# K and V in whole-group transfers, the first x tiles transposed on TensorE, and loads moved at a block change

## The chip, the core and the metric

The kernel runs on one core of one Trainium2 chip. The metric is the device time of one execution in microseconds (us). Engines are named as the profile names them: PE is TensorE (PEld its weight loads), DVE is VectorE, ACT is ScalarE, POOL is GpSimd, SP is SyncE. SP issues every DMA of this kernel from one queue (q1 on the page of the kernel before, 161.12 of the 162.59 MB moved; the rest is instructions), in program order; "SPq" is that queue.

## The reference

Two independent attention blocks, A and B, of the same shape. Each projects x to queries, attends to a cached K and V, and projects back; the two results stand side by side in the output.

```python
# for each of the two blocks; all inputs bf16
B, Sq, D = 8, 144, 640          # batches, queries per batch, model width
H, Sk, Dh = 32, 512, 128        # heads, cached keys, head width
q = (x @ wq).reshape(B, Sq, H, Dh).transpose(0, 2, 1, 3)
scores = einsum("bhqd,bhkd->bhqk", q, k_cache) * Dh ** -0.5
p = softmax(scores)
o = einsum("bhqk,bhkd->bhqd", p, v_cache)
out = o.transpose(0, 2, 1, 3).reshape(B, Sq, H * Dh) @ wo
# result: concatenate([out_A, out_B], axis=-1)
```

K and V are the bulk of the data: 8 x 32 x 512 x 128 bf16 elements, 33.5 MB each for each block.

## The kernel before

The work is cut into 64 **groups**, numbered 0 to 63: one batch, eight heads. Groups 0 to 31 are block A, 32 to 63 block B. For a group, PE projects x to queries, computes the scores (144 queries are 128 "main" and 16 "remainder"; the remainders of all eight heads share one tile), DVE and ACT do the softmax, PE transposes the probabilities, multiplies with V, and later multiplies with wo. Projections by wo ("out-projection") serve as filler between the steps of later groups.

The program declares each operation with what it reads and writes. A static scheduler in the same file then orders every engine's instructions before the program is built. So an edit to the loads can also move instructions on the compute engines.

Every load goes to SP. x is needed transposed, and the DMA transposes it; so is K. K and V come four heads at a time:

```python
NK = 4      # K buffers of 4 heads each
NV = 6      # V buffers of 4 heads each

def load_xT(blk, half):             # half of the 1152 tokens: 576
    ...
    for c in range(NCH):            # NCH = 5 slices of 128 of D = 640
        def f(e, c=c):
            return e.dma_start_transpose(xT_sb[:, c, t0:t1], xf[t0:t1, c * 128:(c + 1) * 128])
        S.add("sp", f, writes=[("xT", half, c)], ...)

def load_kv(blk, b, g):
    for s2 in range(2):             # two 512 KB chunks for K, two for V
        h0 = 8 * g + 4 * s2
        kslot = kv_ctr[0] % NK
        vslot = kv_ctr[0] % NV
        ...
        ksrc = kc[b, h0:h0 + 4].rearrange("h k d -> (h k) d")
        vsrc = vc[b, h0:h0 + 4].rearrange("h (p c) d -> p h (c d)", p=128)
        # K: dma_start_transpose(kt_sb[:, kslot, :], ksrc); V: dma_start(v_sb[:, vslot], vsrc)
```

This is when the other loads are issued (`before(g, f)` puts load f ahead of group g):

```python
before(0, lambda: load_xT(0, 0))                  # A's first x half, first of all
before(0, lambda: load_wq(0, 0))                  # then a quarter of A's wq
for g in range(1, NG):
    before(g, lambda g=g: load_wq(0, g))
...
for blk in range(2):
    for b in range(NB):
        ...
        for g in range(NG):
            attention_group(blk, b, g, gi, fill, heads_done)
            gi += 1
            if blk == 0 and b == NB - 1:
                load_wq(1, g)                     # B's wq, a quarter after each of A's last groups
        if blk == 0 and XH == 2 and b == BPH - 1:
            load_xT(1, 0)
        if blk == 0 and b == NB - 1:
            load_xT(1, XH - 1)                    # B's second x half, exactly at the block change
            queues[0].extend(outproj_ops(blk, NB))
            for hg in range(NHG):                 # B's four wo quarters, all after A's last out-projection
                queues[0].append((1, -1, 0, None, lambda hg=hg: do_load_wo(1, hg), NB - 1))
```

## Time and profile before

| what | value | where it is read |
|---|---|---|
| time, median of the 4 runs known then | 789.9 us (786.13 to 790.65) | the runs |
| PE busy | 747.3 us of a span of 787.2 us | the page, part 1 |
| PE busy, 25 to 100 us | 65.46 of 75 us, DMA at 264 GB/s | busy time by windows |
| PE busy, 375 to 400 us (block change) | 20.69 of 25 us | busy time by windows |
| PE busy, 450 to 475 us (B's wo) | 23.04 of 25 us | busy time by windows |
| first projection matmul | 13.67 us | timeline of PE |

The page of the kernel before, its span, its first part (busy time of each engine, share of the span, instructions) and its fourth (shares of the chain of waits that ended last):

```profile
span 787.2 us, 23122 instructions
PE 747.3 (95%) x9088; PEld 565.6 (72%) x9088; DVE 719.9 (91%) x1858; ACT 613.1 (78%) x1957; POOL 0.7 (0%) x6
PE 84%; DMA 9%; DVE 4%; SPq 1%; ACT 1%; issue 0%; ACTq 0%
```

PE bounds the kernel as a whole. Only about 40 us of the span are idle on PE, and they lie in a few places. The windows view of the kernel before shows those places. Its columns are the stretch in us and its length, then the busy time and instruction count of PE, PEld, DVE, ACT and POOL, then the granted clock of PE as a share of full speed, the DMA share, and the GB/s moved:

```profile
25.00:100.00 75.00, 65.46 (x782) 48.54 (x783) 66.14 (x170) 56.12 (x179) 0.00 (x0) 0.98 1.11 264
375.00:400.00 25.00, 20.69 (x236) 14.81 (x235) 20.44 (x55) 17.32 (x55) 0.00 (x0) 0.97 1.09 235
450.00:475.00 25.00, 23.04 (x249) 15.99 (x247) 19.89 (x51) 17.27 (x57) 0.00 (x0) 1.00 1.07 273
```

The longest waits of PE, from the waits view of the kernel before (who waited for what: us in total, times, longest):

```profile
PE ps_q L396 <- DMA wq_sb<-in_A_wq_dram: 13.7, 1, 13.7
PE ps_s L425 <- DMA kt_sb<-in_B_k_cache_dram: 5.4, 2, 4.3
```

Why these two are long is in the timeline of the SP queue (start, how long the issue held the queue, operation, what it moves, how many). At the start five transposes of x hold the queue before wq gets its turn; at the block change five more hold it for 10.24 us before B's first K:

```profile
0.80 6.46 SPq L315 DMA_TRANSPOSE xT_sb<-in_A_x_dram  x5
7.31 0.58 SPq L294 DMA_DIRECT2D wq_sb<-in_A_wq_dram  x1
7.94 5.48 SPq L335 DMA_TRANSPOSE kt_sb<-in_A_k_cache_dram  x1
...
380.39 10.24 SPq L315 DMA_TRANSPOSE xT_sb<-in_B_x_dram  x5
390.73 5.51 SPq L335 DMA_TRANSPOSE kt_sb<-in_B_k_cache_dram  x2
```

A good clock for progress is the burst of eight small "remainder" score matmuls, one burst per group.

Groups 40 to 60 took 11.3 us each. In groups 0 to 8, K landed only 0.0 to 2.5 us before the scores that read it; later about 6.5 us before. So the first 120 us run at the pace of the DMA, and the rest does not.

### The profile page before, as it was taken

The page shows a single profiled execution, that of the slowest core. Times are in us where ns is not written, and L with a number is a line of the kernel's source. Part 1 is how long each engine was busy: PE and PEld are TensorE (multiplying, and loading weights), DVE is VectorE, ACT ScalarE, POOL GpSimd, SP SyncE. Part 2 cuts the span into 40 slices and gives each one's busy share as a digit, 9 for nine tenths or more (in the row PEclk, how much of TensorE's full clock was granted, in tenths as well). Part 3 has the DMA queues.
Part 4 walks back from the last instruction along what each step waited for, and adds up shares of the span by engine and source line. Part 5 has one row for each costly group of instructions (what it writes and reads, how often), then busy time and mean ns, then how long its engine had stood idle before and what let it go on. Part 6 is the DMA issues. An engine that isn't in the chain of part 4 may idle for free.

```text
span 787.2 us, 23122 instructions
## 1 busy us (share of the span) xinstructions
PE 747.3 (95%) x9088; PEld 565.6 (72%) x9088; DVE 719.9 (91%) x1858; ACT 613.1 (78%) x1957; POOL 0.7 (0%) x6
## 2 busy tenths in 40 slices
PE   2789899999999999999979999999999999999997
PEld 1567667778777777778757767777777778787864
DVE  2799899989999999999969879999999999999992
ACT  1678678778888888888868768888888888888873
POOL 0000000000000000000000000000000000000000
PEclk9999999999999999999999999999999999999999
DMA  7999999998999888899999899988989787889820
GB/s 185 285 236 292 253 253 231 215 230 192 200 221 194 192 196 190 188 229 272 235 227 230 234 267 244 217 186 196 192 190 192 196 185 199 189 194 194 188 34 18
DMA packets 362476, 162.59 MB, mean 207 GB/s; under 512 B 281216, under 2 KB 357248, under 8 KB 362368
## 3 DMA queue, kind: packets, MB, share of 16 engines
q1 hardware_dynamic: 362368, 161.12, 91.2%
q8 instruction: 72, 1.18, 0.7%
q14 instruction: 36, 0.29, 0.1%
HBM read 88.08 MB, written 2.95 MB: 116 GB/s over the span
## 4 chain that ended last, share of the span: by engine, by line
PE 84%; DMA 9%; DVE 4%; SPq 1%; ACT 1%; issue 0%; ACTq 0%
PE ps_q L396 19%; PE ps_o L531 15%; PE ps_out L578 14%; PE ps_pt L504 13%; PE ps_s L483 13%; DMA kt_sb<-in_A_k_cache_dram 5%; PE ps_s L425 4%; PE ps_out L593 4%; DMA kt_sb<-in_B_k_cache_dram 2%; DVE nm_sb L355 2%; PE ps_pt L450 2%; PE ps_q L578 1%; DMA wo_sb<-in_B_wo_dram 1%; DMA wq_sb<-in_A_wq_dram 1%; SPq L315 1%; DVE p_sb L376 1%
## 5 line engine op out<-in xcount | busy, mean ns | idle before, releaser
L359 ACT ACTIVATE p_sb<-ps_s,nm_sb 128x512 bf16<-128x512 f32 x576 | 397.2, 696 | 59.5 <-DVE nm_sb L355 44.2
L355 DVE TENSOR_REDUCE nm_sb<-ps_s 128x1 f32<-128x512 f32 x576 | 383.7, 678 | 26.2 <-PE ps_s L483 17.2
L396 PE MATMUL ps_q<-xT_sb,wq_sb 128*128 128x144 bf16 x2560 | 205.2, 228 | 15.4 <-DMA wq_sb<-in_A_wq_dram 13.7
L396 PEld LDWEIGHTS ps_q<-xT_sb,wq_sb 128*128 128x128 bf16 x2560 | 173.2, 99 | 50.3 <-DMA wq_sb<-in_A_wq_dram 13.7
L520 DVE COPY ptg_sb<-ps_pt 128x1024 bf16<-128x1024 bf16 x256 | 174.7, 685 | 21.6 <-PE ps_pt L504 19.2
L483 PE MATMUL ps_s<-kt_sb,qt_sb 128*128 128x512 bf16 x512 | 184.6, 382 | 7.6 <-ACT p_sb L359 4.3
L376 DVE TENSOR_SCALAR p_sb<-p_sb,rr_sb 128x512 bf16<-128x512 bf16 x576 | 180.2, 345 | 1.4
L531 PE MATMUL ps_o<-ptg_sb,v_sb 128*128 128x144 bf16 x2048 | 171.3, 227 | 0.7 <-DVE ptg_sb L465 0.4
L531 PEld LDWEIGHTS ps_o<-ptg_sb,v_sb 128*128 128x128 bf16 x2048 | 138.8, 98 | 35.8 <-DVE ptg_sb L520 10.8
L504 PE MATMUL ps_pt<-id_sb,p_sb 128*128 128x128 bf16 x2048 | 156.0, 220 | 2.9 <-DVE p_sb L376 2.8
L504 PEld LDWEIGHTS ps_pt<-id_sb,p_sb 128*128 128x128 bf16 x2048 | 132.0, 114 | 24.0 <-DVE p_sb L376 10.7
L407 ACT ACTIVATE qt_sb<-ps_q 128x288 bf16<-128x288 f32 x256 | 106.7, 417 | 53.3 <-PE ps_q L396 50.3
L578 PE MATMUL ps_out<-wo_sb,otm_sb 128*128 128x512 bf16 x512 | 131.4, 379 | 0.9 <-DMA wo_sb<-in_B_wo_dram 0.9
L544 ACT CAST otm_sb<-ps_o 128x256 bf16<-128x256 f32 x256 | 94.9, 371 | 45.9 <-PE ps_o L531 42.1
L359 ACT ACTIVATION_READ_ACCUMULATOR p_sb<-ps_s,nm_sb 128x1 f32 x576 | 120.3, 209 | 0.0
L578 PEld LDWEIGHTS ps_out<-wo_sb,otm_sb 128*128 128x128 bf16 x512 | 48.5, 98 | 44.9 <-issue 1.3
L483 PEld LDWEIGHTS ps_s<-kt_sb,qt_sb 128*128 128x128 bf16 x512 | 47.6, 98 | 24.5 <-ACT p_sb L359 10.4
L371 DVE RECIPROCAL rr_sb<-rs_sb 128x2 f32<-128x2 f32 (+1 forms) x320 | 49.9, 156 | 3.3 <-ACT p_sb L359 2.5
L545 ACT CAST otr_sb<-ps_o 128x32 bf16<-128x32 f32 x256 | 50.4, 197 | 0.0
L425 PE MATMUL ps_s<-kt_sb,qt_sb 128*32 128x512 bf16 x512 | 39.8, 388 | 5.9 <-DMA kt_sb<-in_B_k_cache_dram 5.4
L593 PE MATMUL ps_out<-wo_sb,otm_sb 128*128 128x128 bf16 x512 | 38.8, 219 | 0.0
L593 PEld LDWEIGHTS ps_out<-wo_sb,otm_sb 128*128 128x128 bf16 x512 | 32.3, 98 | 7.4 <-issue 2.5
(25 smaller groups left out, 135.9 us busy)
## 6 DMA issues: line engine op xcount, KB each, us to landing
v_sb<-in_A_v_cache_dram SPq DMA_DIRECT2D x64, 512.0 KB, 4.4
v_sb<-in_B_v_cache_dram SPq DMA_DIRECT2D x64, 512.0 KB, 4.4
wq_sb<-in_A_wq_dram SPq DMA_DIRECT2D x4, 1280.0 KB, 7.5
wo_sb<-in_A_wo_dram SPq DMA_DIRECT2D x4, 1280.0 KB, 8.2
wq_sb<-in_B_wq_dram SPq DMA_DIRECT2D x4, 1280.0 KB, 7.5
wo_sb<-in_B_wo_dram SPq DMA_DIRECT2D x4, 1280.0 KB, 8.2
out_dram<-ost_sb SPq DMA_DIRECT2D x16, 160.0 KB, 3.6
kt_sb<-in_A_k_cache_dram SPq DMA_TRANSPOSE x64, 5.9
```

Of the source, the lines that this page charges most:

```text
L355: return v.tensor_reduce(nm_sb[:, ts:ts + 1], ps_s[:, sbank, :], AXL.X, ALU.max, negate=True)
L359: return a.activation(p_sb[:, pslot, :], ps_s[:, sbank, :], ACTF.Exp, bias=nm_sb[:, ts:ts + 1], scale=1.0, accum_out=rs_sb[:, ts:ts + 1])
L376: return v.tensor_scalar(p_sb[:, pslot, :], p_sb[:, pslot, :], rr_sb[:, ts:ts + 1], None, ALU.mult)
L396: ins = t.matmul(ps_q[:, uu * SQ:(uu + 1) * SQ], wq_sb[:, c, h * 128:(h + 1) * 128], xT_sb[:, c, b * SQ:(b + 1) * SQ], start=(c == 0), sto ...
L407: return a.mul(qt_sb[:, gs, 2 * pi:2 * pi + 2, off:off + SQ], ps_q[:, 0:2 * SQ].rearrange("p (u q) -> p u q", u=2), SCALE,)
L483: return t.matmul(ps_s[:, sbank, :], qt_sb[:, gs, u, qoff:qoff + 128], kt_sb[:, slot, (u % 4) * SK:(u % 4 + 1) * SK], start=True, stop=True,)
L504: ins = t.transpose(ps_pt[:, kpt, (uu * 4 + c) * 128:(uu * 4 + c + 1) * 128], pv[:, c, :], id_sb[:],)
L520: return v.tensor_copy(dst, src)
L531: ins = t.matmul(ps_o[:, uu * SQ:(uu + 1) * SQ], v_sb[:, slot, u % 4, c * 128:(c + 1) * 128], ptg_sb[:, gs, u, c, :], start=(c == 0), stop ...
L544: a.copy(otm_sb[:, bs, h0:h0 + 2, :], src[:, :, 0:128])
L578: ins = t.matmul(acc[:, 0:512], lhs(h), wo_sb[:, h, 0:512], start=(h == 0), stop=(h == H - 1))
L593: ins = t.matmul(acc[:, 0:D2], lhs(h), wo_sb[:, h, 512:D], start=(h == 0), stop=(h == H - 1))
```

## The change

It has three parts that can be switched separately, and I use letters for them:

- **X**: the first 256 tokens of A's x come by one plain DMA (320 KB) and are transposed on PE, so that wq need not wait behind five DMA transposes. The other 320 tokens of the half still come by five DMA transposes, but after the first K and V.
- **K**: K and V come eight heads (1 MB) at a time, in two K and three V buffers of twice the size. The total buffer size stays.
- **R**: loads of B are retimed. B's second x half moves 12 groups later in the program (from the block change to group 44), B's wq quarters one group later, and each wo quarter of B is issued right after A's last reader of the old one rather than all four at the end. The scheduler then places them: in the SP queue of the changed kernel the x half stands before and after K of group 40, and of the wq quarters only the last has changed its place, to behind K of group 32.

A third output staging buffer, checks at build time that a buffer holds what is expected, and a new semaphore numbering of the DMAs come with it. The cut diff:

```diff
+KV_HEADS = 8
+NK, NV = 2, 3
+NOS = 3
+WQB_LEAD = 2
+XT_PE_TILES = 2
 ...
-    NK = 4
-    NV = 6
-    NOS = 2
 ...
+        def load_x_pe():
+            # one plain DMA of 256 tokens into the output staging buffer, then
+            # ten PE transposes by the identity and two evictions by DVE
+            ...
+                        ins = t_.transpose(ps_pt[:, kpt, j * 128:(j + 1) * 128],
+                                           stage[:, t, c * 128:(c + 1) * 128], id_sb[:])
 ...
-            for s2 in range(2):
-                h0 = 8 * g + 4 * s2
+            for s2 in range(8 // KV_HEADS):
+                h0 = 8 * g + KV_HEADS * s2
 ...
-        before(0, lambda: load_xT(0, 0))
-        before(0, lambda: load_wq(0, 0))
+        if NXA:
+            before(0, load_x_pe)
+            before(0, lambda: load_wq(0, 0))
+            if BPH * SQ > NXA:
+                before(1, lambda: load_xT(0, 0, skip=NXA))
 ...
+        for g in range(NG):
+            before(max(last_g[(0, g)] + 1, first_g[(1, g)] - WQB_LEAD), lambda g=g: load_wq(1, g))
+        if XH == 2:
+            before(max(last_half[(0, 1)] + 1, first_half[(1, 1)] - NG), lambda: load_xT(1, 1))
 ...
-                    if blk == 0 and b == NB - 1:
-                        load_wq(1, g)
-                if blk == 0 and b == NB - 1:
-                    load_xT(1, XH - 1)
 ...
+                for k, it in enumerate(passb):
+                    queues[0].append(it)
+                    for hg in range(NHG):
+                        if ((hg + 1) * 8 - 1) // OPB_HEADS == k:
+                            queues[0].append((1, -1, 0, None, lambda hg=hg: do_load_wo(1, hg), NB - 1))
```

With every switch of the changed kernel set back, the program that it builds has the same instructions and waits, in the same order on every engine, as the kernel before. So X, K and R are the whole of the change.

## The prediction

> **What bounds the kernel now.** TensorE: the page gives PE 95% busy, and the chain of waits is 84% PE. The windows table shows three regimes.
> - To 125 us: DMA bound. The first matmul starts at 13.67 us, after a 13.7 us wait on A's wq. From 25 to 125 us the DMA share is 1.10 to 1.16 at 244 to 276 GB/s, PE is busy 21.0 to 23.9 of 25 us, and groups of 8 heads (timeline, one remainder-score burst each) are mostly 11.9 to 13.6 us apart.
> - 125 to 750 us: PE bound, 25.0 of 25 us; late groups are 11.3 us apart; DMA 180 to 210 GB/s.
> - Two dents: 375 to 400 us (PE 20.7 of 25, a 4.3 us wait on K), where transposes of B's second x half stand before K in the queue (380 to 390 us), and 450 to 475 us (PE 23.0), where B's four wo loads do.
>
> Counting matmul starts later than their line's median, the excess over steady state is about 38 us up to 125 us, 5 us at the block change, 2 us at wo.
>
> **What the change does.**
> 1. First x: five 576-token DMA transposes (issued 0.8 to 7.3 us) become one plain 320 KB load, ten PE transposes (about 56 ns each) and evictions (about 0.7 us each, DVE idle). wq goes second instead of sixth and should land near 8 us, not 13.6. The other 320 tokens still go through the transposing DMA, behind K and V. Estimate: 4 to 5 us gained; the DMA-bound stage ends that much earlier, and this reaches the kernel's end.
> 2. K and V in 1 MB transfers. [...] Here the 512 KB transfers already stand back to back on saturated engines: I expect 0 to 3 us. The price: K of group i+2 starts only when all scores of group i are done. Now K's second half lands about 6.5 us before its scores in steady state; a 1 MB K takes about 2.5 us longer, so slack falls to 2 to 5 us: free in steady state, thin where weights load.
> 3. B's second x half moves 12 groups later, B's wq one or two groups, each B wo follows its last reader. The block-change stall nearly goes, but wq adds about 4 us of DMA to each of four groups with thin K slack: net 2 to 4 us. The four wo still stand before one, now whole, K: 0, give or take 2.
> 4. A third output buffer and the buffer assertions: nothing.
>
> PE work[...] is unchanged; the gain is removed idle time: 4.5 + 1 + 3 = about 8 us.
>
> **Predicted:** 782 us, 774 to 788 eight times in ten. Faster by over 2%: 0.16; within 2%: 0.81; slower by over 2%: 0.03.
>
> **What would show it.** Step 1: first projection matmul near 8 to 9 us, first scores near 14 instead of 16.7; A's wo loads end 3 to 6 us before the 104.3 of now. Step 2: unchanged 250 to 275 GB/s from 25 to 100 us; PE still 25.0 of 25 in steady state. Step 3: no x transposes near 385 us; the wait on B's K under 2 us; PE over 23 of 25 us in 375 to 400.
>
> **What would make it wrong.** If 1 MB transfers raise the saturated DMA rate, groups 0 to 8 shorten by about 1 us each and the gain passes 15 us. If the two whole-group K slots arrive late (waits on K every group), or an in-order V or wo issue blocks K, it is slower. If the rebuilt static order is worse on PE, 0.1 us per group is 6 us.

4.5 + 1 + 3 comes to 8.5, called about 8 us, and leads from 789.9 to 782 us. The 1 of step 2 was a guess within its 0 to 3 us.

Where the other figures stand in the kernel before: its 128x128 PE transposes begin 56 ns apart (a burst of eight at 600.03 us, the next matmul at 600.48), and a DVE copy of 128x1024 takes 685 ns. The 2.5 us are an estimate, from the 2.6 us (median) for which a 512 KB transpose of B's K holds the queue. The 4 us are one too: 1280 KB of wq at the 338 GB/s moved from 450 to 462 us, where wo quarters of the same size load, would take 3.9 us.

## More of the kernel before

In the timeline of PE of the kernel before, the first line is the first projection; the others are the bursts of groups 4, 8, 28 and 40:

```profile
13.67 1.38 PE L396 MATMUL ps_q<-xT_sb,wq_sb 128*128 128x144 bf16 x10 [13.67 <-DMA wq_sb<-in_A_wq_dram]
...
72.19 0.62 PE L425 MATMUL ps_s<-kt_sb,qt_sb 128*32 128x512 bf16 x8
...
120.86 0.61 PE L425 MATMUL ps_s<-kt_sb,qt_sb 128*32 128x512 bf16 x8
...
348.63 0.61 PE L425 MATMUL ps_s<-kt_sb,qt_sb 128*32 128x512 bf16 x8
...
498.65 0.61 PE L425 MATMUL ps_s<-kt_sb,qt_sb 128*32 128x512 bf16 x8
```

Groups 4 to 8 took 12.2 us each ((120.86 - 72.19) / 4).

## The result, and the profile after

The changed kernel took 781.73 us (median of 11 runs, 779.37 to 782.44), against 788.88 us for the kernel before (15 runs, 785.85 to 791.7). The ratio is 0.9903, with a 95% interval of 0.9888 to 0.9918. Here and below, a ratio is the mean time of one kernel's fast runs over the mean of the other's in the same rounds, so it is not quite the ratio of the medians that are quoted. When the same file was run again it took 779.34 us (4 runs) against 788.14 us, ratio 0.9891 [0.9867, 0.9915].

The page of the changed kernel, the same three lines:

```profile
span 779.8 us, 22892 instructions
PE 752.0 (96%) x9098; PEld 568.8 (73%) x9098; DVE 719.1 (92%) x1860; ACT 614.8 (79%) x1957; POOL 0.7 (0%) x6
PE 86%; DVE 7%; ACT 2%; DMA 2%; SPq 1%; issue 0%; ACTq 0%
```

PE has ten matmuls more (the x transposes) and is 7.4 us shorter in span. DMA fell from 9% of the last chain to 2%. The windows view of the changed kernel, the same stretches:

```profile
25.00:100.00 75.00, 67.14 (x806) 51.12 (x807) 66.67 (x172) 56.60 (x181) 0.00 (x0) 1.00 1.14 286
375.00:400.00 25.00, 25.00 (x299) 18.72 (x297) 24.22 (x67) 20.21 (x67) 0.00 (x0) 1.00 1.09 270
450.00:475.00 25.00, 24.24 (x277) 17.13 (x276) 16.96 (x47) 15.51 (x48) 0.00 (x0) 1.00 1.12 265
```

Two things stand out. The rate in the first window rose from 264 to 286 GB/s, which I had predicted not to happen. And the dent at the block change is gone: 25.00 of 25 us. The waits view of the changed kernel has for the same causes:

```profile
PE ps_q L465 <- DMA wq_sb<-in_A_wq_dram: 4.3, 1, 4.3
PE ps_pt L366 <- DMA ost_sb<-in_A_x_dram: 3.8, 1, 3.8
...
PE ps_s L498 <- DMA kt_sb<-in_B_k_cache_dram: 0.4, 1, 0.4
```

The timeline of the SP queue of the changed kernel, at the start and at the block change:

```profile
0.81 0.46 SPq L353 DMA_DIRECT2D ost_sb<-in_A_x_dram  x1
1.33 0.45 SPq L310 DMA_DIRECT2D wq_sb<-in_A_wq_dram  x1
1.83 9.06 SPq L396 DMA_TRANSPOSE kt_sb<-in_A_k_cache_dram  x1
...
11.56 6.41 SPq L341 DMA_TRANSPOSE xT_sb<-in_A_x_dram  x5
18.02 0.58 SPq L310 DMA_DIRECT2D wq_sb<-in_A_wq_dram  x1
...
378.99 5.30 SPq L396 DMA_TRANSPOSE kt_sb<-in_B_k_cache_dram  x1
384.34 0.57 SPq L310 DMA_DIRECT2D wq_sb<-in_B_wq_dram  x1
```

wq is issued at 1.33 instead of 7.31 us. But look at the x transposes: the five of 320 tokens hold the queue for 6.41 us, no less than the five of 576 tokens did before (6.46 us). X moved this time to a later place; it did not save it. (The five of 82 KB each stand behind a K and a V, the five of 147 KB stood on an empty queue. Whether the time is a cost per transfer or a queue that was full is open.)

The timeline of PE of the changed kernel, the first projection and the bursts of groups 4, 8, 28 and 40:

```profile
9.34 1.38 PE L465 MATMUL ps_q<-xT_sb,wq_sb 128*128 128x144 bf16 x10 [4.31 <-DMA wq_sb<-in_A_wq_dram]
...
69.61 0.61 PE L498 MATMUL ps_s<-kt_sb,qt_sb 128*32 128x512 bf16 x8
...
114.61 0.62 PE L498 MATMUL ps_s<-kt_sb,qt_sb 128*32 128x512 bf16 x8
...
345.85 0.61 PE L498 MATMUL ps_s<-kt_sb,qt_sb 128*32 128x512 bf16 x8
...
491.35 0.61 PE L498 MATMUL ps_s<-kt_sb,qt_sb 128*32 128x512 bf16 x8
```

The gain can be followed along the groups:

| burst of group | before | changed | earlier by | changed, run again | earlier by |
|---|---|---|---|---|---|
| 0 | 22.5 | 16.9 | 5.6 | 15.8 | 6.7 |
| 4 | 72.2 | 69.6 | 2.6 | 65.6 | 6.6 |
| 8 | 120.9 | 114.6 | 6.3 | 110.6 | 10.3 |
| 28 | 348.6 | 345.9 | 2.7 | 341.3 | 7.3 |
| 40 | 498.7 | 491.3 | 7.4 | 486.7 | 12.0 |
| end of span | 787.2 | 779.8 | 7.4 | 775.1 | 12.1 |

From group 4 to 8 the changed kernel takes 11.25 us a group, already its steady pace (groups 40 to 60: 11.3 us). Some 3 to 4 us of the lead at group 8 are gone at group 28. In the static order of the eight-head kernels about 2 us of work stands behind that mark instead of ahead of it (worked out from the durations of the instructions on both sides of the burst), so at least half of this is no loss. The same holds at groups 0 and 4, so the lead over the kernel before is smaller there than the table says. (Kernels with the same chunk size have the mark at the same place and can be compared directly.) After group 28 the block change and the wo loads bring another 4.7 us. Nothing is gained or lost after group 40.

The two traces of the same program differ by 4.7 us at the end, 4.0 us of it already at group 4. The section on the clock below comes back to that.

### The profile page after: what moved, and what is told of

It reads as the page before. It is cut to its first block, busy times and chain, and to the rows that moved or that the text cites. A ratio compares the mean times of both kernels' runs of the same rounds, so it can differ in the third digit from the quotient of the medians.

```text
span 779.8 us, 22892 instructions
## 1 busy us (share of the span) xinstructions
PE 752.0 (96%) x9098; PEld 568.8 (73%) x9098; DVE 719.1 (92%) x1860; ACT 614.8 (79%) x1957; POOL 0.7 (0%) x6
## 4 chain that ended last, share of the span: by engine, by line
PE 86%; DVE 7%; ACT 2%; DMA 2%; SPq 1%; issue 0%; ACTq 0%
PE ps_q L465 19%; PE ps_out L667 17%; PE ps_o L613 16%; PE ps_pt L582 14%; PE ps_s L559 13%; PE ps_s L498 5%; DVE nm_sb L415 4%; PE ps_pt L525 2%; ACT p_sb L420 2%; DVE p_sb L441 2%; DVE ptg_sb L594 1%; DMA kt_sb<-in_B_k_cache_dram 1%; PE ps_q L667 1%; DMA wq_sb<-in_A_wq_dram 1%; SPq L696 1%; DVE ptg_sb L536 0%
## 5 line engine op out<-in xcount | busy, mean ns | idle before, releaser
L667 PE MATMUL ps_out<-wo_sb,otm_sb 128*128 128x128 bf16 (+1 forms) x1024 | 170.1, 299 | 0.0
L582 PE MATMUL ps_pt<-id_sb,p_sb 128*128 128x128 bf16 x2048 | 157.8, 220 | 0.7 <-DVE p_sb L441 0.6
L536 DVE COPY ptg_sb<-ps_pt 128x256 bf16<-128x256 bf16 x128 | 30.8, 282 | 2.8 <-PE ps_pt L525 2.4
L525 PE MATMUL ps_pt<-id_sb,p_sb 128*128 128x128 bf16 x256 | 25.2, 221 | 1.0 <-DVE p_sb L441 1.0
```

The lines of the kernel that those rows point to most:

```text
L582: ins = t.transpose(ps_pt[:, kpt, (uu * 4 + c) * 128:(uu * 4 + c + 1) * 128], pv[:, c, :], id_sb[:],)
L667: ins = t.matmul(acc[:, 0:c1 - c0], lhs(h), wo_sb[:, h, c0:c1], start=(h == 0), stop=(h == H - 1))
```

## The experiments

Each experiment is an edit of the changed kernel unless said otherwise. The letters in the table say which parts are in. Kernels of one call share the runs of the kernel before, whose medians were 789.07, 790.71 and 788.14 us in calls 1, 2 and 3. The three calls ran on three different chips, so between calls only the ratios are compared. All were correct.

| kernel | parts in | call | median us | ratio to before [95%] |
|---|---|---|---|---|
| changed | X K R | first | 781.73 | 0.9903 [0.9888, 0.9918] |
| u_kv4 | X R | 1 | 784.43 | 0.9949 [0.9918, 0.9981] |
| u_xdma | K R | 1 | 786.21 | 0.9962 [0.9936, 0.9988] |
| u_noretime | X K | 1 | 784.86 | 0.9945 [0.992, 0.997] |
| u_xb | X K, R but for one load | 1 | 782.4 | 0.9909 [0.9883, 0.9935] |
| w_warm | X K R + warm-up | 2 | 784.91 | 0.9928 [0.9903, 0.9954] |
| w_late3 | X K R, rest of x later | 2 | 784.31 | 0.9925 [0.99, 0.995] |
| w_late3_warm | both | 2 | 784.77 | 0.9931 [0.991, 0.9953] |
| o_kv8 | K | 2 | 788.4 | 0.9974 [0.9951, 0.9997] |
| c_after | X K R (same file again) | 3 | 779.34 | 0.9891 [0.9867, 0.9915] |
| c_keep | X K R + filler matmuls | 3 | 780.27 | 0.9896 [0.9876, 0.9916] |
| c_late3_keep | rest of x later + filler matmuls | 3 | 782.0 | 0.9925 [0.9903, 0.9946] |
| o_x | X | 3 | 791.11 | 1.0039 [1.0015, 1.0063] |

My theory after the first look: X gives about what the trace shows at group 0; K gives something too, because the DMA rate rose; R removes the block-change stall. The rival to the first two: the start is bound by DMA anyway, so a lead from X is given back, and only the faster transfers of K count.

### u_kv4: the chunk size put back

```diff
-KV_HEADS = 8
-NK, NV = 2, 3
+KV_HEADS = 4
+NK, NV = 4, 6
```

> The changed kernel with K and V back in 4-head chunks (4 K slots, 6 V slots), all else as changed. Changed kernel: ratio 0.990 to before (781.7 us). Theory A (the gain is idle time taken out at the start by the PE-transposed x and at the block change by the later x half; the larger chunk adds little and costs K slack): 779 to 783 us, ratio 0.986 to 0.991; K lands again in halves, the last about 6.5 us before its remainder scores in steady state. Rival B (the 1 MB chunk is what pays: DMA moved 280 to 291 GB/s from 25 to 100 us in the changed kernel against 255 to 276 before): 785 us or more, ratio 0.994 or more, and 25 to 100 us falls back to about 264 GB/s.

It took 784.43 us: about half of the gain is lost (0.51% left of 0.97%). The windows view of u_kv4, 25 to 100 us:

```profile
25.00:100.00 75.00, 62.60 (x758) 47.26 (x759) 61.97 (x156) 52.63 (x166) 0.00 (x0) 0.97 1.11 261
```

The rate is back at 261 GB/s, and PE busy is 4.5 us less than in the changed kernel in this stretch. Groups 0, 4 and 8 come at 17.5, 72.6 and 121.6 us: 5.0 us ahead of the kernel before at group 0, 0.4 us *behind* at group 4, 0.7 behind at group 8. So X's lead is there at first and gone by group 4 when the chunks are small.

### u_xdma: the first x by DMA transpose again

```diff
-XT_PE_TILES = 2
+XT_PE_TILES = 0
 ...
         else:
-            before(0, lambda: load_wq(0, 0))
             before(0, lambda: load_xT(0, 0))
+            before(0, lambda: load_wq(0, 0))
```

> The changed kernel with the first x again loaded by five DMA transposes before wq, all else as changed. Theory A: the first projection matmul returns to about 13.5 us and 3 to 5 us are lost: 785 us, ratio 0.994 to 0.996. Rival B: at most 1.5 us lost, ratio 0.990 to 0.992.

It took 786.21 us, so with K and R in, X is worth 0.59 points (0.97 less 0.38), some 4.7 us. Group 0 comes at 21.3 us, group 4 at 74.4, group 8 at 119.4. The changed kernel is 4.4, 4.8 and 4.8 us earlier at these marks in its first trace, and 5.5, 8.8 and 8.8 us in its second. Here the lead of X is *not* given back: with large chunks (276 GB/s in this kernel from 25 to 100 us) it survives past group 8.

### u_noretime and u_xb: B's loads put back, all of them or one

u_noretime puts back all three retimings, u_xb only the x half:

```diff
 # u_xb, and in u_noretime too
-            before(max(last_half[(0, 1)] + 1, first_half[(1, 1)] - NG), lambda: load_xT(1, 1))
+            before(last_half[(0, 1)] + 1, lambda: load_xT(1, 1))
 # u_noretime only
-WQB_LEAD = 2
+WQB_LEAD = 3
 ...
-                for k, it in enumerate(passb): ...      # one wo load after each reader
+                queues[0].extend(passb)
                 queues[0].extend(tail_)
+                for hg in range(NHG):
+                    queues[0].append((1, -1, 0, None, lambda hg=hg: do_load_wo(1, hg), NB - 1))
```

> The changed kernel with the times of block B's loads put back (second x half at the block change, wq one group earlier, wo all after the remainder projection). Theory A: the stall at 380 to 400 us returns, PE about 20.7 of 25 us there: 5 to 6 us lost, 787 us, ratio 0.996 to 0.998. Rival B: 0 to 2 us lost, as the 1 MB K is requested early enough.

> The changed kernel with only block B's second x half moved back to the block change; wq and wo of B stay as changed. If the x half alone is the stall (theory A): 4 to 6 us lost, about the same as with all three put back, ratio 0.995 to 0.998. If the wq and wo times carry it: 0 to 1.5 us lost, ratio 0.990 to 0.992.

u_noretime took 784.86 us: R as a whole is worth 0.42 points beside X and K (0.97 less 0.55), or about 3.3 us. u_xb took 782.4 us: the x half by itself costs 0.06 points by this comparison (0.18 against the control), which its interval does not tell from nothing, nor from some 2 us. In the windows view, PE busy from 375 to 400 us is 24.02 us in u_noretime and 25.00 in u_xb, against 20.69 in the kernel before. (It is 23.72 in o_kv8, below, which has K alone, 22.63 in u_kv4, which has R but not K, and 22.42 in o_x, below, which has neither. So two single traces without K and R differ by 1.7 us here.) I had put the block-change stall down to the x transposes ahead of K, because that is what stands in the queue. Moving them back did not bring the stall back in this window. It brought a smaller one into the next. The windows view from 400 to 425 us, of the changed kernel and then of u_xb:

```profile
400.00:425.00 25.00, 25.00 (x314) 19.16 (x311) 24.79 (x65) 21.52 (x69) 0.00 (x0) 1.00 0.91 211
400.00:425.00 25.00, 22.85 (x284) 17.33 (x282) 22.63 (x61) 19.31 (x64) 0.00 (x0) 1.00 1.07 257
```

PE waits 3.0 us in all for B's K in u_xb (0.4 in the changed kernel, 5.4 in the kernel before), and groups 28 to 40 take 149.0 us against 145.5. The traced run of u_xb is hardly longer for it, because it had come to group 28 sooner, by 2.7 us (group 4 at 66.9 us against 69.6; see the section on the clock). But traces of other kernels with all of R in take up to 148.9 us for the same groups. So the x half costs something between nothing and about 3 us, and how the dent is shared between K, the x half and the other two retimings stays open.

### o_kv8 and o_x: one part alone on the kernel before

These two have only K, and only X, with everything else (the staging buffers too) as in the kernel before.

```diff
 # o_kv8: x by DMA first, B's loads as in u_noretime
-NOS = 3
-WQB_LEAD = 2
-XT_PE_TILES = 2
+NOS = 2
+WQB_LEAD = 3
+XT_PE_TILES = 0
 # o_x: as o_kv8, but XT_PE_TILES = 2 and
-KV_HEADS = 8
-NK, NV = 2, 3
+KV_HEADS = 4
+NK, NV = 4, 6
```

> The kernel before with only the chunk changed to 8 heads (x by DMA first, block B's loads as before, two output buffers). From the undone runs: undoing the chunk cost 2.7 us of 7.5, so the chunk alone should gain 2 to 4 us, ratio 0.995 to 0.997, DMA 275 GB/s or more from 25 to 100 us, and the stall at the block change about half as long as the 4.3 us of before. If the chunk pays only together with the earlier start: 0 to 1 us, ratio 0.999 to 1.000.

> The kernel before with only the first x changed (two PE-transposed tiles, wq second in the queue, the rest of x by five DMA transposes before group 1). As predicted it should gain 4 to 5 us, ratio 0.994 to 0.995. From the run with the chunk undone, whose group 4 started at 72.6 us against 72.2 before: with 4-head chunks the stage stays bound by DMA, and the early start is gone by group 4: 0 to 1 us, ratio 0.998 to 1.000.

K alone took 788.4 us, a gain of 0.26%. X alone took 791.11 us, a *loss* of 0.39%; its interval does not reach 1. The windows view of o_kv8, 25 to 100 us:

```profile
25.00:100.00 75.00, 66.77 (x772) 51.22 (x781) 66.92 (x171) 55.90 (x178) 0.00 (x0) 0.95 1.13 278
```

The same window of o_x:

```profile
25.00:100.00 75.00, 60.98 (x747) 46.91 (x759) 61.55 (x155) 52.59 (x166) 0.00 (x0) 0.98 1.09 259
```

K alone gives the higher rate, X alone does not. Where X alone loses its lead is in the timelines of o_x. First its SP queue, with the moved x transposes and the second quarter of wq behind them:

```profile
12.60 6.33 SPq L341 DMA_TRANSPOSE xT_sb<-in_A_x_dram  x5
18.97 0.58 SPq L310 DMA_DIRECT2D wq_sb<-in_A_wq_dram  x1
19.60 5.39 SPq L396 DMA_TRANSPOSE kt_sb<-in_A_k_cache_dram  x1
```

Then its PE, the bursts of groups 4 and 8:

```profile
71.62 0.62 PE L498 MATMUL ps_s<-kt_sb,qt_sb 128*32 128x512 bf16 x8
...
121.91 0.62 PE L498 MATMUL ps_s<-kt_sb,qt_sb 128*32 128x512 bf16 x8
```

Group 0 came at 17.1 us, 5.4 us ahead of the kernel before. At group 4 it is 0.6 us ahead, at group 8 it is 1.0 us behind. In the kernel before, K of group 1 (the first K of the second group) was issued at 19.21 us; in o_x at 19.60. So the queue needs as long for its work up to there, only in another order, and the groups after the first wait for the queue. The stage ends no earlier either: A's last wo landed at 105.2 us in o_x, at 104.3 in the kernel before.

One caution: the profiled run of o_x is its fastest (788.51 of 788.51 to 794.33 us). Its trace ends no later than that of the kernel before. So it shows that the lead is given back, but not where the median's loss of 3 us comes from. The slower runs of o_x list mean granted clocks down to 0.982; that the clock is the cause is a guess.

With o_kv8 and o_x, seven of the eight combinations have been measured:

| parts | gain, % of the time before |
|---|---|
| none | 0 |
| X | -0.39 |
| K | 0.26 |
| X K | 0.55 |
| K R | 0.38 |
| X R | 0.51 |
| X K R | 0.97 (1.09 when run again) |

Singly X and K sum to -0.13; together they give 0.55. Each entry carries an interval of about 0.25 to 0.3 either way, so a difference of two carries about 0.35 to 0.4. The interplay of X and K, 0.68 points from three such entries (about 0.4 either way), is larger than that; more than half of it rests on the loss of X alone, whose size is not explained. The effect of R differs among its three contrasts (0.42 beside X and K, 0.12 beside K, 0.90 beside X), and these I can't tell apart well. R alone was not run.

### The clock of PE at the start

The first scores came at 16.2 us where I had predicted 14, although the first projection was on time (9.34 us). One reason is the order: with eight-head chunks the static order puts all four blocks of projections (ten matmuls each) ahead of the first scores, with four-head chunks two (first scores at 11.0 us in o_x and u_kv4). K had landed at 13.0 us. And the projections themselves are slow there. In the timeline of PE of the changed kernel, ten matmuls of the same form at 26.94 us and at 29.87 us:

```profile
26.94 1.41 PE L465 MATMUL ps_q<-xT_sb,wq_sb 128*128 128x144 bf16 x10
...
29.87 0.79 PE L465 MATMUL ps_q<-xT_sb,wq_sb 128*128 128x144 bf16 x10
```

1.41 against 0.79 us for the same work. The clock column of the profile does not show this: it reads 1.00 there, and its first record in this trace begins at 29.8 us. But where the column reads 0.50, from 26.3 to 29.7 us in the kernel before, the same ten matmuls take 1.41 us too (at 28.34 us). So I take it that PE ran at half speed up to 29.8 us.

Theory: the half-speed start costs several us, and work for PE ahead of its first projections gains them. That such work brings the full clock sooner was a guess. Rival: the start waits for data anyway, and a faster PE only waits more. At the same time I tried to move the rest of x further back, to take its queue time out of the first groups.

```diff
 # w_warm: 20 identity matmuls before the x transposes, 44 after, into an unused score bank
+            warm(20, [("ident",)])
 ...
+            warm(44, [("xTa", 0)])
 # w_late3: three x tiles by PE instead of two, the other 192 tokens before group 6
-XT_PE_TILES = 2
+XT_PE_TILES = 3
 ...
-                before(1, lambda: load_xT(0, 0, skip=NXA))
+                before(6, lambda: load_xT(0, 0, skip=NXA))
 # w_late3_warm: both
```

> The changed kernel plus 64 matmuls of the identity into a score bank that is not in use yet (20 before and 44 after the transposes of x), in the time in which PE waits for x and wq; the order of all other instructions is the same. Cold-PE theory: in the changed kernel's profile ten 128x144 matmuls took 1.38 us up to 28 us and 0.79 after, so PE ran its first 20 us at half speed and group 1 began 3.8 us after its K had landed; warmed up, the first projections take 0.8 us per ten, the ledger at group 4 falls from 32.3 to about 29 to 30 us, and 2 to 3 us are gained: ratio 0.986 to 0.988. Rival (the start waits for DMA, not for PE): 0 to 0.7 us, ratio 0.989 to 0.991.

> The changed kernel with three x tiles (384 tokens) transposed on PE and the rest (192 tokens, five DMA transposes) loaded before group 6 instead of before group 1. In the changed kernel those five stand before wq of group 1 and hold the queue from 11.6 to 17.9 us. If they delay group 1: wq lands 5 to 6 us earlier than 24.4, group 1 begins 3 to 5 us earlier than 34.1, and 3 to 4 us are gained in all: ratio 0.985 to 0.987. If group 1 waits for cold PE and not for its data: under 1 us, ratio 0.989 to 0.991.

> Both together, meant to beat both kernels. If both hold and add up: 5 to 6 us below the changed kernel, about 776 us, ratio 0.982 to 0.985. If only one of the two matters, the same as that one alone.

w_warm took 784.91, w_late3 784.31, w_late3_warm 784.77 us. None beats the changed kernel. In w_warm the clock did rise early: its projection at 13.71 us takes 0.80 us. But half-speed stretches came back. The windows view of w_warm, with the granted clock third from the right:

```profile
24.00:37.00 13.00, 9.68 (x114) 6.86 (x115) 10.37 (x26) 9.32 (x30) 0.00 (x0) 1.00 1.12 279
37.00:40.40 3.40, 3.10 (x25) 2.86 (x26) 2.75 (x9) 1.35 (x5) 0.00 (x0) 0.50 1.16 250
40.40:50.60 10.20, 7.93 (x100) 5.78 (x98) 8.03 (x20) 7.44 (x24) 0.00 (x0) 1.00 1.23 309
```

PE is busy for 9.68 of 13 us, then runs at 0.50 for 3.4 us, then at 1.00 again. Another such dip comes at 50.6 us, 13.65 us after the first by the trace. Dips of this length are found in the first groups of most kernels here (o_kv8 at 41.4 and 55.1 us, u_xdma at 42.0 and 55.7, w_late3 at 35.8 and 49.5), where PE is not full (62.60 of 75 us in u_kv4, 66.77 in o_kv8 and 67.90 in u_xdma from 25 to 100 us); some last twice as long (u_kv4, 22.5 to 29.3 us). The kernel before has one at 26.3 us and one more at 398.4 us (0.50 to 401.8 us), the latter after its 4.3 us wait at the block change. In the first trace of the changed kernel and in that of u_xb there are none between the rise of the clock and the last 3 us.

That led to the last theory: keep PE busy with filler through the first groups, and the dips go. c_keep puts four identity matmuls wherever the filler queue has nothing to offer until A's first wo has been issued; c_late3_keep does so on w_late3. The changed kernel was run with them as a control.

```diff
+KEEP_WARM = 4
 ...
             if fill_state[0] % FILL_STRIDE == 0:
-                pop_filler()
+                if not pop_filler() and not wo_loaded:
+                    warm(KEEP_WARM)
```

> The changed kernel once more, as the control of this call: the ratios of the first call (0.9903) and of the later ones were taken at other times. If 0.990 holds, the undone and added parts may be read against it: 0.988 to 0.992. If the control comes out at 0.993 or more, the differences of the warm and late variants from the changed kernel are nothing.

> The changed kernel plus short bursts of 4 identity matmuls (into the output-projection bank, unused until then) wherever the static order has PE wait in groups 0 to 3, and 24 at the start. Clock theory: in the profiles of groups 0 to 4 the granted clock falls to half for 3.4 us once or twice (37.0 and 50.6 us with the warm-up, 41.4 and 55.1 with the chunk alone)[...]; kept busy, no dip up to 75 us, group 4 starts at 66 to 67 us instead of 69.6, and 2 to 3 us are gained over the control: ratio lower than the control's by 0.003. Rival (the groups are paced by VectorE's 11.3 us and the dips lie in its shadow): the same as the control within 0.0015, or slower.

> The same bursts with three PE-transposed x tiles and the rest of x loaded before group 6; the candidate to beat both kernels. In the late-x profile group 1 began at 30.8 us instead of 34.1 but the lead was down to 1.2 us at group 4 and gone at group 8. If the dips took it: group 4 at 65 to 66 us, ratio lower than the control's by 0.004 to 0.006. If not: equal to the late-x run, no better than the control.

c_keep had no dip from 11.4 us to the last 2 us, and its four runs lie within 779.48 to 780.69 us. But its median, 780.27, is not below the control's 779.34. Filler makes the time steadier, perhaps; it makes it no shorter. The trace of the control had no dip either, so this pair does not test the dips. c_late3_keep and w_late3 do (in different calls), and have the same ratio, 0.9925. The rival fits: group 0 of c_keep came at 14.3 us, 1.5 us ahead of the control, but group 1 at 30.1 us, as in the control; and K of groups 4 to 6 landed only 0.7 to 1.2 us before its scores, against 3.9 to 6.1 in the first trace of the changed kernel. c_late3_keep took 782.0 us. Its lead at group 4 (65.3 us, against 65.6 in the control) is gone at group 8 (112.3 against 110.6), where the late x transposes stand.

The control brought a result of its own. In its timeline of PE:

```profile
13.94 1.38 PE L465 MATMUL ps_q<-xT_sb,wq_sb 128*128 128x144 bf16 x10 [0.50 <-ACT qt_sb L476]
15.82 0.62 PE L498 MATMUL ps_s<-kt_sb,qt_sb 128*32 128x512 bf16 x8 [0.50 <-ACT qt_sb L476]
...
65.62 0.61 PE L498 MATMUL ps_s<-kt_sb,qt_sb 128*32 128x512 bf16 x8
...
110.61 0.62 PE L498 MATMUL ps_s<-kt_sb,qt_sb 128*32 128x512 bf16 x8
```

The clock rose at 15.7 us here and at 29.8 us in the first trace of the same program. At group 4 they are 4.0 us apart, and from group 4 to 8 both take 45.0 us. At the end they are 4.7 us apart. So when the clock rises differs from run to run. This run's first projection also came 1.05 us earlier (8.29 against 9.34 us), but u_xb and u_noretime settle more. Up to group 8 their programs are the same as this one, they begin within 0.06 us of it, and K of group 1 landed at 28.5 us in all three:

| trace | first projection, us | PE at half speed before group 4 | group 4, us |
|---|---|---|---|
| c_after | 8.29 | to 15.7 us | 65.6 |
| u_xb | 8.30 | to 23.7 us | 66.9 |
| u_noretime | 8.24 | to 17.7 us, and 13.65 us in three dips | 70.6 |

The longer PE was at half speed, the later group 4 came, by up to 5.0 us. So the clock can be a large part of the spread among runs of one kernel. That it is all of it isn't shown: a late PE and its dips can also be the effect of data that came late.

## Why the prediction was right or wrong

The total was right: 782 us predicted, 781.73 measured. Its parts were less so, and they met in the sum.

**Bounds.** Right. Three regimes, with two dents, was what the experiments then took apart. The idle time that was removed lay in the start (2.7 us of lead at group 28 in the first trace, 7.3 in the second) and at the block change and wo (4.7 us in both).

**Step 1, the first x by PE: 4.5 us.** The size was right in the changed kernel (0.59 points, about 4.7 us, from u_xdma), but the reason that I gave was wrong. The step that failed reads "the DMA-bound stage ends that much earlier, and this reaches the kernel's end". In o_x the early start didn't make the end of that stage earlier: group 0 came 5.4 us ahead, group 4 only 0.6 us, and A's last wo landed at 105.2 us against 104.3. The DMA had no less to do: the x transposes held the queue for 6.33 us there (6.41 in the changed kernel) instead of 6.46. X alone lost 0.39%. It clearly paid only where K and R were both in (0.59). Beside K alone it gave 0.29 points (0.55 less 0.26), within the interval of such a difference, and what it gives beside R alone is not known, as R alone was not run. With K in, the DMA no longer sets the pace after the first groups: in groups 0 to 8 K lands 3.2 to 7.0 us before its scores, against 0.0 to 2.5 us before. Of the signs, the first projection near 8 to 9 us came (9.34, and 8.29 in the control), and A's last wo landed at 95.7 us instead of 104.3, 8.6 us earlier and more than the 3 to 6 that I gave. The first scores near 14 us did not come (16.2 us): four blocks of projections stood ahead of them instead of two, each of 1.38 us on a half-speed PE instead of 0.80. I had counted neither.

**Step 2, the 1 MB transfers: 0 to 3 us, taken as 1.** K alone gave 0.26%, about 2 us, within the range. Beside X and R it gave 0.46 points (0.97 less 0.51), about 3.6 us. The step that failed is "unchanged 250 to 275 GB/s from 25 to 100 us". The rate rose to 286 (292 in the control), and to 271 to 294 in the other kernels with large chunks; the kernels with small chunks stayed at 259 to 264. My argument was that the engines were saturated already (DMA share 1.11), so that size did not matter. But the same share of 1.11 stands beside 264 GB/s in the kernel before and 292 in the control. So here the share did not tell how much was moved. I had said that a higher rate would bring more than 15 us. It did not. Once K lands early, groups 2 to 4 are paced by the compute engines, at 11.3 to 11.4 us a group, near the 11.2 us of DVE work in one (719.1 us over 64 groups). Past that, as I read it, more rate has nothing to give. What in the larger transfers raises the rate was not tested.

The price that I gave was right: K's slack in steady state fell from about 6.5 us to 3 to 6 us, I had said 2 to 5. It touched zero at groups 16, 29, 30 and 37, without waits on K that add up.

**Step 3, B's loads: 2 to 4 us, taken as 3.** Right in size: 0.42 points or about 3.3 us (u_noretime against the changed kernel). From the traces, groups 28 to 40 took 145.5 us instead of 150.0, of which part may be K's (o_kv8: 148.6; but o_x, with neither K nor R, took 148.5). The signs came: no x transposes near 385 us, 0.4 us of wait on B's K, PE busy 25.00 from 375 to 400 us. The step named the x half as the cause of the stall, and that is shown at most in part. u_xb put it back, and the window from 375 to 400 us stayed full, while 2.15 us of PE's time were lost from 400 to 425. K without R took the first window from 20.69 to 23.72 us, but o_x, with neither, has 22.42. So some of what I had booked under step 3 may belong to step 2; single traces do not say how much. Which of the other two retimings counts was not separated. The wo dent shrank a little (23.04 to 24.24 us from 450 to 475, but 25.00 became 24.24 from 475 to 500), inside my "0, give or take 2".

**Step 4, buffers and checks: nothing.** No run isolates this. The identical programs with all switches back show that the checks and the numbering cost no instruction.

So the sum held because one omission offset another; that it came within 1 us was luck. I had left out the rate, which raises the gain, and the half-speed PE at the start and the giving-back of X's lead, which lower it, and the second is largely undone by the first.

## What to carry to other kernels

Starting earlier in the stage that the queue bounds gained nothing here while the queue had no less to do and was no faster (X alone: 5.4 us ahead at group 0, A's last wo at 105.2 us against 104.3, 0.39% lost): compare when the *last* load of the stage is issued, not when the first compute starts. X and K were worth -0.39% and 0.26% alone, and 0.55% together, so test a change also beside what relieves the next limit. And before blaming a transfer that stands ahead of a late one in the queue, put it back alone, and look past the stretch in which the wait was: here it moved to the next one (u_xb: PE busy 25.00 of 25 us from 375 to 400 us, 22.85 from 400 to 425).
